# Attention and two MLPs in one launch: the written-out order and engines of the first two thirds of the steps replaced, after new step costs and a price on changes between kinds of TensorE product

## The chip, the cores and the metric

The kernel runs on one core of one Trainium2 chip. The metric is the device time of one execution in microseconds (us); less is better. The time before is the median of three runs.

## The reference

Three layers follow one another. `x` is the output of one layer and the input of the next.

```python
# attention: 4 batches, 8 heads, 576 positions, 64 per head
scores = scale * np.matmul(q, k.transpose(0, 1, 3, 2))
masks = np.stack([mask_plain if h < H // 2 else mask_dil for h in range(H)], axis=0)
scores = np.where(masks[None, :, :, :], scores, -1000000000.0)
attn = np.exp(scores - np.max(scores, axis=-1, keepdims=True))
attn = attn / (np.sum(attn, axis=-1, keepdims=True) + 1e-09)
x = np.matmul(attn, v)                 # then laid out as 2304 tokens x 512
# first MLP: 512 -> 1024 -> 512
h = x @ w_in
solu = h * softmax(h)
x = (solu - mean) / np.sqrt(var + 1e-06) * g_ln @ w_out
# second MLP: 512 -> 2048 -> 512
h = x @ w_in
x = (h * (1.0 / (1.0 + np.exp(-1.702 * h)))) @ w_out
```

`mask_plain` lets a position see the last 32 positions, `mask_dil` every fourth of the last 128. The weights arrive as 64-bit floats.

## The kernel before

**Attention.** The window is narrow, so scores are made only near the diagonal. The work is cut into 20 units n = 0 to 19, five per batch: four of two heads each, and a fifth, small one (n = 4, 9, 14, 19) for the last 64 positions of all heads. A unit goes through these steps: `att_s` makes the scores s on TensorE out of many small products (64 rows by 32 columns of the array) that follow, in the first two batches, a product of the identity with the mask; `att_max`, `att_sub` and `att_exp` work on VectorE and ScalarE; `att_sum` and `att_norm` give t on VectorE and GpSimd; `att_t` transposes t on TensorE into ptp; `att_p` copies it into diag (pt for a small unit); `att_x` multiplies with v on TensorE into xt (128 rows by 64 columns); `att_y` copies xt into the ring xr of layer input. The trace counts each of these narrow products twice.

**First MLP.** 18 token tiles of 128 rows. To keep precision every operand is split into a high and a low half, and three products are made (high by high, high by low, low by high): `moe_xh` and `moe_xl` split x, `moe_h` makes h in two halves of 12 matmuls of 512 columns each. Then follow a row maximum nm (`moe_max`, VectorE), an exponential (`moe_exp`, ScalarE), the product with h into e (`moe_solu`, VectorE), which gives h's PSUM room back, the layer norm, eight transpositions lt (`moe_lt`), their split into ln_t, and per group of three tiles the products y (`moe_y`, 24 matmuls of 384 columns each).

**Second MLP.** Three passes of 768 tokens. A two-by-two scheme with seven products instead of eight makes hx and hz (`h_prod`) and, after the activation, ox and oz (`o_prod`); sums of blocks are made before and after on VectorE, and again all operands are split in halves (gs holds the split activations, wo and w the weights). Both weight matrices of this layer are summed, split and written to DRAM (wdq, wdo) during the first MLP and read back later.

**What sets the order.** Every step is a `Work` with one or more engines that can do it and a cost in us for each (lines 946 to 1300, where `add` is called). `ORDER` is a list of the numbers of all 2,394 works. The works of one engine stand in its queue in the order of this list. `PICKS` says for a work whether it takes the second or third of its engines. `Plan.replay` (line 81) walks the queues with the costs as they are written and with rules for hops, DMA and instruction fetch; it decides in what order the works are emitted and how many filler products (`stir`, line 270) are put ahead of a product that by this reckoning has to wait. The filler works on a bank that the next product overwrites, so it only keeps TensorE at work. Each engine executes its queue strictly in this order, and waits where an input isn't there. All loads and stores go through SyncE's queue, which is in ORDER as well.

**TensorE's room.** Scores of four-head units and h share two PSUM tiles (`A`); small scores, transpositions, xt, lt and y share four banks (`B`).

Of the kernel before, what the change touches and what calls it, by code (L numbers as in the profile page):

```python
# [49 lines left out]
COLD, EARLY, LATE_RATE = 7.5, 60.0, 320e3  # L50
# [14 lines left out]
class Plan:  # L65
# [15 lines left out]
    def replay(self):  # L81
# [15 lines left out]
        port, land, lanes, ld, mms, left = 0.0, 0.0, [0.0] * LANES, 0, [], len(order)  # L97
        while left:
            best = None
            for e in QUEUES:  # L100
                if at[e] >= len(queues[e]):
                    continue
                w = queues[e][at[e]]
# [27 lines left out]
            if e == "PE":  # L131
# [7 lines left out]
                end, cost = t, w.cost * (2 if t < COLD else 1)  # L139
                for _ in range(w.mm):  # L140
# [38 lines left out]
def attention_moe_kernel(ctx, tc, qk, qk_last, v, v_last, masks, w_in, w_out, g_ln, w2_in, w2_out, out):  # L179
    nc = tc.nc  # L180
# [823 lines left out]
    for i in range(NTILE):  # L1004
# [24 lines left out]
        w = add(r, "ACT", 1.4, lambda i=i: moe_var(i), [w, z])  # L1029
        w = add(r, "POOL", 0.62, lambda i=i: moe_rs(i), [w])  # L1030
        w = add(r, "ACT", 1.4, lambda i=i: moe_ln(i), [w], port=True,
# [37 lines left out]
    for k in (1, 2, 3):  # L1069
        w_after = [end[n] for n in range(4)] if k < 3 else [closed]  # L1070
        raw, hl = (("raw", k), ("hl", k)) if k < 3 else ("raw", "hl")
        for n, u in enumerate(PARK[k]):
# [8 lines left out]
            for i in range(3):  # L1081
                w = add(r, "POOL", 0.41 if i else 0.69, lambda u=u, i=i: unit_sum(u, i, nc.gpsimd), [w], port=True,
                        also=[("DVE", 0.29 if i else 0.42, lambda u=u, i=i: unit_sum(u, i, nc.vector))])
            lo_ = None
            for part in range(2):
                fin = part == 1

                def split(copy, k=k, u=u, part=part):
# [4 lines left out]
                        also=[("DVE", 0.42 if fin else 0.35, lambda s=split: s(nc.vector.tensor_copy)),  # L1093
# [251 lines left out]
def plan_sequence():  # L1345
# [74 lines left out]
ORDER = [4, 1, 78, 79, 80, 81, 19, 88, 89, 90, 5, 8, 57, 58, 59, 60, 3, 263, 68, 91, 92, 93, 94, 262, 82, 61, 62, 0, 47, 48,  # L1420
# [239 lines left out]
```

## Time and profile before

| | us |
|---|---|
| median of 3 runs (lowest, highest) | 647.04 (646.61, 647.83) |
| profiled execution | 646.25 |
| span in it, first to last instruction | 644.5 |
| TensorE busy with matmuls | 626.5 (97%) |
| VectorE, ScalarE, GpSimd busy | 459.9, 324.2, 257.1 |
| first product of the first MLP starts at | 39.4 |
| first product of the second MLP starts at | 268.3 |
| first product of the second pass of the second MLP starts at | 402.8 |

The first line tells the metric; all other numbers are of one profiled execution, which is 0.8 us shorter than the median. The span leaves out 1.75 us around it. A timeline row gives start, length, engine, line, operation and tile; the bracket at its end tells how long the engine stood idle before it and what ended that. Lines are those of the kernel before; in the changed kernel the same statements stand four lines later.

### The profile page before, as it was taken

To read this page: it belongs to the slowest core of one execution; us is meant where nothing else is said; L and a number is where in the kernel's file an instruction comes from. 1 tells how busy PE (TensorE), PEld (TensorE's weight loads), DVE (VectorE), ACT (ScalarE), POOL (GpSimd) and SP (SyncE) were. 2 spreads that over 40 slices of the span, in tenths; PEclk is the share of its full clock that TensorE was granted. 3 is DMA by queue.
4 is the path that set the end of the run, shared out by engine and by line. 5 is a ranking of instruction groups with operands and counts; after the bars stand their busy time and mean duration, and the time that the engine had idled before them with its cause. 6 is when DMAs were issued, how large, how long until landed. Compare 5 with 4: busy or idle time off the path is not lost.

```text
span 644.5 us, 13119 instructions
## 1 busy us (share of the span) xinstructions
PE 626.5 (97%) x5065; PEld 588.8 (91%) x5065; DVE 459.9 (71%) x817; ACT 324.2 (50%) x706; POOL 257.1 (40%) x282
## 2 busy tenths in 40 slices
PE   6889999999999999999999999999999999999997
PEld 3678789889899899999999899999999999999997
DVE  3878998876787976663779969434678963448795
ACT  4689977776475564714547443322454213243331
POOL 2557546454444434655353244204123240026220
PEclk9889999999999999999999999999999999999999
DMA  8899326763667448635988998677898966868584
GB/s 319 319 376 406 116 101 221 255 212 131 216 241 255 178 149 271 235 124 174 321 291 298 343 344 296 236 253 261 275 331 261 330 206 216 290 255 296 186 262 163
DMA packets 65006, 161.36 MB, mean 250 GB/s; under 512 B 6960, under 2 KB 28592, under 8 KB 64944
## 3 DMA queue, kind: packets, MB, share of 16 engines
q1 hardware_dynamic: 64944, 160.53, 71.4%
q8 instruction: 40, 0.66, 0.4%
q14 instruction: 22, 0.18, 0.1%
HBM read 126.42 MB, written 34.08 MB: 249 GB/s over the span
## 4 chain that ended last, share of the span: by engine, by line
PE 82%; DVE 7%; DMA 4%; ACT 3%; issue 2%; POOL 1%; SPq 0%; POOLq 0%; DVEq 0%; ACTq 0%
PE y L638 15%; PE hz L762 15%; PE oz L844 14%; PE hx L762 11%; PE h L557 11%; PE ox L844 9%; PE lt L618 2%; DMA wo<-wdo 2%; DMA wdq<-hl_('q', 7, 1)_0_4305 1%; PE s L292 1%; PE xt L406 1%; DVE e L577 1%; PE ptp L377 1%; DVE gs L812 1%; DMA qk<-in_qk_dram 1%
## 5 line engine op out<-in xcount | busy, mean ns | idle before, releaser
L809 ACT CAST gs<-g 128x384 fp32r<-128x384 f32 x115 | 57.9, 513 | 87.7 <-DVE g L805 37.0
L638 PE MATMUL y<-ln_t,wo_h 128*128 128x384 f32 x384 | 98.4, 337 | 0.0
L762 PE MATMUL hz<-yc,ws 128*128 128x384 f32 x492 | 97.6, 335 | 0.0
L812 DVE TENSOR_TENSOR gs<-g,gs 128x384 fp32r<-128x384 f32 x133 | 80.2, 621 | 21.8 <-ACT gs L809 15.9
L762 PEld LDWEIGHTS hz<-yc,ws 128*128 128x128 f32 x492 | 86.3, 188 | 0.1
L762 PE MATMUL hx<-yc,ws 128*128 128x384 f32 x369 | 74.4, 335 | 0.0
L638 PEld LDWEIGHTS y<-ln_t,wo_h 128*128 128x128 f32 x384 | 69.0, 188 | 0.7
L812 POOL TENSOR_TENSOR gs<-g,gs 128x384 fp32r<-128x384 f32 x35 | 38.8, 1113 | 72.1 <-ACT gs L809 70.4
L762 PEld LDWEIGHTS hx<-yc,ws 128*128 128x128 f32 x369 | 64.8, 188 | 0.2 <-ACT p L767 0.2
L638 PE MATMUL y<-ln_t,wo_l 128*128 128x384 f32 x192 | 64.3, 335 | 0.0
L805 POOL TENSOR_TENSOR g<-g,g 128x384 f32<-128x384 f32 x25 | 28.4, 1142 | 80.2 <-DVE g L805 44.9
L557 PE MATMUL h<-wi_h,xh 128*128 128x512 f32 x144 | 59.0, 410 | 0.9 <-DVE e L577 0.9
L844 PE MATMUL ox<-gs,wo 128*128 128x384 f32 x288 | 55.7, 337 | 1.5 <-DVE gs L812 1.2
L557 PE MATMUL h<-wi_l,xh 128*128 128x512 f32 x144 | 56.6, 393 | 0.0
L557 PE MATMUL h<-wi_h,xl 128*128 128x512 f32 x144 | 56.6, 393 | 0.0
L844 PE MATMUL oz<-gs,wo 128*128 128x384 f32 x288 | 55.2, 335 | 0.1
L844 PE MATMUL oz<-gs,w 128*128 128x384 f32 x288 | 53.4, 336 | 0.0
L844 PEld LDWEIGHTS ox<-gs,wo 128*128 128x128 f32 x288 | 50.2, 188 | 3.0 <-DVE gs L812 2.5
L844 PEld LDWEIGHTS oz<-gs,wo 128*128 128x128 f32 x288 | 50.3, 188 | 0.7 <-DVE gs L812 0.7
L844 PEld LDWEIGHTS oz<-gs,w 128*128 128x128 f32 x288 | 50.1, 188 | 0.7 <-DVE gs L812 0.6
L805 DVE TENSOR_TENSOR g<-g,g 128x384 f32<-128x384 f32 x71 | 43.5, 622 | 5.9 <-ACT g L795 3.4
L795 ACT ACTIVATE g<-g 128x384 f32<-128x384 f32 x72 | 35.0, 520 | 22.6 <-DVE g L771 14.3
(420 smaller groups left out, 1203.2 us busy)
## 6 DMA issues: line engine op xcount, KB each, us to landing
wo<-wdo SPq DMA_DIRECT2D x48, 512.0 KB, 5.5
ws<-wdq SPq DMA_DIRECT2D x41, 512.0 KB, 5.4
w<-wdo SPq DMA_DIRECT2D x72, 256.0 KB, 5.1
ws<-wdq SPq DMA_DIRECT2D x41, 384.0 KB, 4.8
qk<-in_qk_dram SPq DMA_DIRECT2D x14, 528.0 KB, 7.3
v<-in_v_dram SPq DMA_DIRECT2D x14, 512.0 KB, 7.5
out_dram<-ob SPq DMA_DIRECT2D x11, 384.0 KB, 4.7
w_t<-in_w_in_dram SPq DMA_DIRECT2D x8, 512.0 KB, 7.6
```

The source lines that it names most:

```text
L292: nc.tensor.matmul(ps[QB * j:QB * j + QB, h, m * KW:m * KW + KW], q_[rows, c:c + QB], k_[rows, c:c + KW], start=not masked, stop=not maske ...
L377: nc.tensor.transpose(ps[:, j * P:j * P + P], t[:, 2 * j:2 * j + 2, :].rearrange("p m k -> p (m k)"), ident)
L406: nc.tensor.matmul(o, vW[4 * b + u][:, h, 4 * c + j, :], x, start=True, stop=True, tile_position=(0, 64 * h))
L557: nc.tensor.matmul(hps[i][:, half, :], x[:, kt, :], w[:, kt, fs], start=(kt == 0 and j == 0), stop=(kt == KT - 1 and j == 2))
L618: nc.tensor.transpose(ps[:, j, :], es[i][:, f * P:f * P + P], ident)
L638: nc.tensor.matmul(yps[g, dm][:, 0:TG].rearrange("p (t n) -> p t n", t=GT), w[:, f, ds_], x[:, :, f, :], start=(f == 0 and j == 0), stop=( ...
L762: nc.tensor.matmul(ps[:, 0:TB2], quad_weights(p, q, m, kk, a), yc2[m][:, x, kk, :], start=(m < 4 and kk == 0 and i == 0), stop=(kk == 1 an ...
L795: nc.scalar.activation(g_tile(q, 0, 0) if (half, b) == (0, 0) else src, src, AF.Gelu_apprx_sigmoid)
L805: eng.tensor_tensor(o_block(jj, *o), o_block(jj, *x), o_block(jj, *y_), op)
L809: copy(gsp[jj, m][:, 0], o_block(jj, half, b))
L812: eng.tensor_tensor(gsp[jj, m][:, 1], o_block(jj, half, b), f32(gsp[jj, m][:, 0]), ALU.subtract)
L844: nc.tensor.matmul(ps, w, gsp[jj, m][:, x], start=m < 4 and first and i == 0, stop=last and i == 2, skip_group_check=True)
```

## The change

The planner's costs and one rule are edited, and ORDER and PICKS are replaced by what a new search over them gave. No step of computation is added or taken away. The rule: when the kind of TensorE work changes from one to the next, 0.095 us are added in `replay`. Kind 2 is a work of 32 matmuls or more (scores and xt), kind 1 one of 2 or 4 (transpositions), kind 0 all others (h, y, hx, hz, ox, oz). Priced are the changes from kind 1 or 2 to 0, and from 0 to 2.

```diff
-COLD, EARLY, LATE_RATE = 7.5, 60.0, 320e3
+COLD, EARLY, LATE_RATE, TURN = 7.5, 60.0, 320e3, 0.095
...
                 end, cost = t, w.cost * (2 if t < COLD else 1)
+                kind = 2 if w.mm >= 32 else int(w.mm in (2, 4))
+                if last and not kind or kind == 2 and not last and len(mms) > 12:
+                    end += TURN
+                last = kind
...
-        w = add(r, "ACT", 1.4, lambda i=i: moe_var(i), [w, z])
-        w = add(r, "POOL", 0.62, lambda i=i: moe_rs(i), [w])
-        w = add(r, "ACT", 1.4, lambda i=i: moe_ln(i), [w], port=True,
+        w = add(r, "ACT", 1.56, lambda i=i: moe_var(i), [w, z])
+        w = add(r, "POOL", 0.55, lambda i=i: moe_rs(i), [w])
+        w = add(r, "ACT", 1.57, lambda i=i: moe_ln(i), [w], port=True,
...
-                w = add(r, "POOL", 0.41 if i else 0.69, lambda u=u, i=i: unit_sum(u, i, nc.gpsimd), [w], port=True,
+                w = add(r, "POOL", 0.43 if i else 0.86, lambda u=u, i=i: unit_sum(u, i, nc.gpsimd), [w], port=True,
...
-                        also=[("DVE", 0.42 if fin else 0.35, lambda s=split: s(nc.vector.tensor_copy)),
+                        also=[("DVE", 0.42 if fin else 0.545, lambda s=split: s(nc.vector.tensor_copy)),
...
-ORDER = [4, 1, 78, 79, 80, 81, 19, 88, 89, 90, 5, 8, 57, 58, 59, 60, 3, 263, 68, 91, 92, 93, 94, 262, 82, 61, 62, 0, 47, 48,
+ORDER = [1, 4, 78, 79, 80, 81, 82, 19, 88, 89, 90, 8, 57, 58, 59, 60, 5, 68, 91, 92, 93, 61, 62, 69, 94, 9, 267, 268, 269,
```

The first 1,600 of the 2,394 numbers of ORDER stand in a new sequence and the last 794 as before; 297 works take another engine. On TensorE the sequence of products is new up to the first product of the second pass of the second MLP, and the same from there to the end. The instructions of VectorE grow from 791 rows to 806, those of ScalarE fall from 568 to 552 and of GpSimd from 272 to 264, where alike neighbours count as one row. The fillers ahead of products fall from 15 to 11. In SyncE's queue the mask now stands first, the scores' operand of unit 1 (one piece of 528 KB) ahead of that of unit 2 (two pieces), and the third and fourth tile of w_in no longer both behind the operand of unit 6.

On TensorE in attention's first batches, the rows between unit 1's product with v and unit 0's or 2's; s is a unit's scores, ptp its transposition, xt its product with v, L274 in the kernel before a filler. Before:

```order
L406 MATMUL xt1_480<-diag0_105,v1_193 64x2x32 x16
...
L274 MATMUL ptp0_507<-ident_b_72 128x512
L377 MATMUL ptp0_507<-ident_67,t0_402 128x128 x4
...
L300 MATMUL s9_521<-mk_104,ident_b_72 128x256
L304 MATMUL s9_521<-qkl1_397 32x64 x16
L406 MATMUL xt3_546<-diag1_106,y1_early_79 64x2x32 x16
...
L292 MATMUL s7_564<-qk6_416 32x64 x32
L377 MATMUL ptp2_600<-ident_67,t2_471 128x128 x4
L406 MATMUL xt0_625<-diag0_105,v0_421 64x2x4x8 x16
```

The same place now:

```order
L410 MATMUL xt1_476<-diag0_105,v1_312 64x2x32 x16
L410 MATMUL xt3_506<-diag1_106,y1_early_79 64x2x32 x16
L381 MATMUL ptp0_529<-ident_67,t0_465 128x128 x4
L381 MATMUL ptp2_535<-ident_67,t2_375 128x128 x4
...
L308 MATMUL s9_542<-qkl1_408 32x64 x16
...
L296 MATMUL s7_564<-qk6_418 32x64 x32
...
L278 MATMUL xt2_608<-ident_b_72 128x512
L410 MATMUL xt2_608<-diag1_106,y1_early_79 64x2x4x8 x16
L410 MATMUL xt0_650<-diag0_105,v0_461 64x2x4x8 x16
```

The two products with v and the two transpositions have moved together ahead of unit 9's scores, four fillers ahead of ptp0 and one ahead of s9 are gone, and one stands ahead of xt2, which now comes before xt0.

On TensorE between the halves of the first MLP's h2 and h1 (names as above). Before:

```order
L557 MATMUL h2_900<-wi_h_95,xl2_808 128x512
L406 MATMUL xt6_998<-diag0_105,v5_820 64x2x32 x16
L292 MATMUL s13_1019<-qk11_806 32x64 x32
L377 MATMUL ptp8_1057<-ident_67,t8_729 128x128 x4
L406 MATMUL xt7_1068<-diag1_106,v6_810 64x2x4x8 x16
L557 MATMUL h1_1089<-wi_h_95,xh1_968 128x512
```

The same place now:

```order
L561 MATMUL h2_902<-wi_h_95,xl2_827 128x512
L381 MATMUL ptp6_986<-ident_67,t6_832 128x128 x4
L410 MATMUL xt7_991<-diag0_105,v6_761 64x2x4x8 x16
L296 MATMUL s13_1014<-qk11_810 32x64 x32
L381 MATMUL ptp11_1052<-ident_67,t11_894 128x128 x4
L410 MATMUL xt6_1060<-diag1_106,v5_836 64x2x32 x16
L561 MATMUL h1_1084<-wi_h_95,xh1_976 128x512
```

The transposition of unit 6, which stood inside h2, has moved to its end, so the full-width h is followed by another full-width product, and the narrow ones come behind that.

On VectorE from unit-tile 3's maximum nm3 to its e3, which frees the room of h3 (ln_t is the split transposition, t14 a small unit's masked scores, wo_l a weight split). Before:

```order
L530 SCALAR_TENSOR_TENSOR wo_l_87<-w1_t_91,g_sb_73,wo_h_86 128x512 x2
L565 TENSOR_REDUCE nm3_1297<-h3_1208 128x1
L324 TENSOR_REDUCE mx13_1327<-t13_1062 128x8
L315 SCALAR_TENSOR_TENSOR t14_1337<-s14_1310,mk_104 128x256
L324 TENSOR_REDUCE mx14_1357<-t14_1337 128x4
L625 CAST ln_t_1300<-lt0_0_1301 128x512
L577 SCALAR_TENSOR_TENSOR e3_1354,mu3_1374<-h3_1208,e3_1354 128x1024
```

The same place now:

```order
L534 SCALAR_TENSOR_TENSOR wo_l_87<-w1_t_91,g_sb_73,wo_h_86 128x512 x4
L544 CAST xh4_1302<-xr_97 128x512
L569 TENSOR_REDUCE nm3_1304<-h3_1209 128x1
L319 SCALAR_TENSOR_TENSOR t14_1339<-s14_1315,mk_104 128x256
L480 SCALAR_TENSOR_TENSOR y1_early_79<-y1_early_79 128x512
L581 SCALAR_TENSOR_TENSOR e3_1354,mu3_1363<-h3_1209,e3_1354 128x1024
```

Between nm3 and e3 stand two rows instead of four; the cast of lt0_0 has gone to ScalarE, where it stands just ahead of the exponential of h3.

## Rows read from the trace of the kernel before

**Rows 1.** The page: busy us of each engine, and the instruction queue.
```profile
PE 626.5 (97%) x5065; PEld 588.8 (91%) x5065; DVE 459.9 (71%) x817; ACT 324.2 (50%) x706; POOL 257.1 (40%) x282
...
q8 instruction: 40, 0.66, 0.4%
```

**Rows 2.** Stretches: length, busy PE, PEld, DVE, ACT, POOL; PEclk, DMA share, GB/s.
```profile
0.00:41.00 41.00, 29.56 (x834) 21.20 (x835) 26.32 (x52) 25.34 (x70) 19.46 (x27) 0.92 0.91 327
...
37.00:40.40 3.40, 3.40 (x85) 2.97 (x69) 2.56 (x4) 3.18 (x5) 1.76 (x2) 0.50 1.02 413
41.00:402.70 361.70, 358.80 (x2865) 330.71 (x2864) 281.55 (x487) 220.30 (x470) 175.58 (x193) 1.00 0.68 239
```

**Rows 3.** Timeline of TensorE in the first 40 us (columns as told above).
```profile
10.29 0.86 PE L292 MATMUL s<-qk 64*32 64x64 f32 x64 [1.62 <-DMA qk<-in_qk_dram]
...
14.80 0.44 PE L377 MATMUL ptp<-ident,t 128*128 128x128 f32 x2 [0.17 <-POOL t L369]
...
20.00 0.58 PE L288 MATMUL s<-mk,ident_b 128*128 128x256 bf16 x2 [2.07 <-DVE mx L327]
...
23.48 1.04 PE L274 MATMUL ptp<-ident_b 128*128 128x512 bf16 x4
...
29.81 1.15 PE L406 MATMUL xt<-diag,v 128*64 128x64 f32 x32 [0.88 <-DVE diag L388]
...
36.66 1.04 PE L292 MATMUL s<-qk 64*32 64x64 f32 x63 [1.83 <-issue]
...
39.40 0.78 PE L557 MATMUL h<-wi_h,xh 128*128 128x512 f32 x1
```

**Rows 4.** Timeline of GpSimd, first norm steps.
```profile
14.13 2.62 POOL L369 TENSOR_TENSOR t<-t,sx 128x256 f32<-128x256 f32 x3 [11.56 <-DVE sx L364]
```

**Rows 5.** Timeline of VectorE ahead of the product with v at 29.81.
```profile
27.44 1.39 DVE L476 SCALAR_TENSOR_TENSOR w_t<-w_t 128x1024 uint32<-128x1024 uint32 x1
...
29.08 0.67 DVE L388 COPY diag<-ptp 64x512 f32<-64x512 f32 x1
```

**Rows 6.** Timeline of TensorE where the kind of product changes.
```profile
53.52 0.39 PE L557 MATMUL h<-wi_h,xl 128*128 128x512 f32 x1
53.84 1.15 PE L406 MATMUL xt<-diag,v 128*64 128x64 f32 x32
...
57.38 0.50 PE L557 MATMUL h<-wi_h,xh 128*128 128x512 f32 x1
57.71 0.40 PE L557 MATMUL h<-wi_l,xh 128*128 128x512 f32 x1
57.95 0.39 PE L557 MATMUL h<-wi_h,xl 128*128 128x512 f32 x1
...
74.95 0.60 PE L618 MATMUL lt<-ident,e 128*128 128x128 f32 x4
75.48 0.65 PE L304 MATMUL s<-qkl 64*32 64x64 f32 x32
...
83.26 1.47 PE L618 MATMUL lt<-ident,e 128*128 128x128 f32 x12
84.57 0.60 PE L377 MATMUL ptp<-ident,t 128*128 128x128 f32 x4
84.93 0.48 PE L557 MATMUL h<-wi_h,xh 128*128 128x512 f32 x1
85.25 0.40 PE L557 MATMUL h<-wi_l,xh 128*128 128x512 f32 x1
```

**Rows 7.** Timeline around the wait at 80.42, three engines.
```profile
77.25 1.12 ACT L571 ACTIVATE e<-h,nm 128x1024 f32<-128x1024 f32 x1
...
79.05 1.22 DVE L577 SCALAR_TENSOR_TENSOR e<-h,e 128x1024 f32<-128x1024 f32 x1
...
80.42 0.47 PE L557 MATMUL h<-wi_h,xh 128*128 128x512 f32 x1 [0.92 <-DVE e L577]
```

**Rows 8.** Timeline of TensorE, a wait in the second MLP.
```profile
361.85 1.16 PE L844 MATMUL ox<-gs,wo 128*128 128x384 f32 x5 [0.57 <-DVE gs L812]
```

More of the change, by code (lines that the diff above doesn't have):

```diff
@@ L96, in replay @@
         free["SP"] = 0.75
-        port, land, lanes, ld, mms, left = 0.0, 0.0, [0.0] * LANES, 0, [], len(order)
+        port, land, lanes, ld, mms, left, last = 0.0, 0.0, [0.0] * LANES, 0, [], len(order), 0
         while left:
@@ L1535 @@
     2353, 2354, 2386, 2387, 2388, 2355, 2390, 2392, 2356, 2357, 2376, 2385, 2389, 2380, 2391, 2393]
-PICKS = {53: 1, 65: 1, 67: 1, 74: 1, 75: 1, 96: 1, 105: 1, 124: 1, 137: 1, 156: 1, 158: 1, 169: 1, 181: 1, 191: 1, 200: 1,
[24 rows of a table removed]
+PICKS = {56: 1, 64: 1, 75: 1, 85: 1, 87: 1, 94: 1, 96: 1, 97: 1, 108: 1, 116: 1, 119: 1, 127: 1, 129: 1, 137: 1, 138: 1,
[26 rows of a table added]
 _INS = ["qk", "qk_last", "v", "v_last", "masks", "w_in", "w_out", "g_ln", "w2_in", "w2_out"]
```

198 rows, old and new, of tables (ORDER, PICKS) are left out of this document.

## The prediction, made before the changed kernel ran

> **What bounds the kernel.** I read the busy times first: TensorE is at work for 97% of the span, no other engine for more than 71% [rows 1]. So the question is where TensorE stands still or runs slowly, and the table of stretches answers that. In the first 41 us it is busy for 29.56, so it idles 11.44; from 41 us to 402.7, where the sequence of its products becomes the old one again, it idles 361.70 - 358.80 = 2.90 us in all [rows 2]. After that nothing is changed on TensorE. The change can therefore win in three places: in the first 41 us, in those 2.90 us, and in products that run longer than they need. The timeline of TensorE shows what the first part consists of [rows 3]: a wait for a load (1.62 us, at 10.29), for a norm step of GpSimd (at 14.80), two stops of about 2 us (at 20.00 and 36.66), a copy of VectorE (0.88, at 29.81). In the stretch from 37.0 to 40.4 the granted clock is 0.50, the lower of its two levels, 1.2 of 2.4 GHz, right after the stop that ends at 36.66.
>
> **The stops.** The one at 36.66 is labelled issue: nothing that the profile shows was missing. The one at 20.00 names a maximum of unit 2, but the product that waits writes unit 5's scores, so I take it for the same thing. Counted along the timeline, 349 matmuls ran before the first of these and 730 before the second. The instruction queue moved 40 packets of 0.66 MB together, 16 KB each, for 5065 + 5065 matmuls and weight loads [rows 1]: 253 instructions a packet, some 127 pairs. 730 - 349 = 381 is three times 127. So TensorE runs out of instructions at a block's end if the narrow products, 63 in 1.04 us, use up a block faster than the next one comes. The product sequence of the changed kernel has the same counts up to 415 matmuls, so the stop at 20.00 stays. The block ends near 478 and 606 fall today into unit 9's scores and into xt0, and no stop is seen there. Now they fall on the last matmuls of xt3, behind xt1, with nothing wide in between, and into xt2. This is the one place where the change puts more narrow products in a row.
>
> **The change part by part.**
> *The first 15 us.* Unit 1's operand of 528 KB now passes unit 2's in SyncE's queue. At 327 GB/s in this stretch [rows 2] 540,672 bytes are 1.65 us, so the wait of 1.62 us at 10.29 goes. But what comes next is ptp of the small unit, at 14.80, and it waits for GpSimd, whose norm starts at 14.13, released by VectorE's reciprocal [rows 4]. That chain stands in the same order on VectorE and ScalarE. Unit 3's norm is now ahead of it in GpSimd's queue; GpSimd had idled for 11.56 us, and three norms take 2.62, so it should be through by then; if not, it costs its 0.9 us. I take 0 for all of this: the gain is given back at 14.80.
> *15 to 39.4 us.* Up to unit 5's scores nothing differs. Then four fillers ahead of ptp0 go, 1.04 us [rows 3], of which I count 0.9, since a matmul's end overlaps with the next one's start; xt3 and ptp2 take their place. So the same set of products (xt1, xt3, ptp0, ptp2, s9, s7) should be through 0.9 us earlier. What is late next is the first product with v after it: today xt0 at 29.81, behind a 1.39 us step on w_in and a 0.67 us copy of VectorE [rows 5]; now xt2, behind the same pair of steps, while the maximum of the small unit that stands between them (29.08 - 27.44 - 1.39 = 0.25) moves behind the copy. Then xt0 follows directly, and its copy on ScalarE now stands behind unit 9's exponential: a new wait, with ptp9, s8 and all else on TensorE queued behind it. I price it like today's in front of xt0, 0.88, so that on waits nothing is won. From there to the first h the units and the stop are the same. My value is 0.9 us earlier at 39.4. From below: 2.5 earlier, if the stop of 1.83 also falls into one of these waits. From above: 0.9 later, if a further stop of 1.83 opens at the block ends named.
> *Changes of kind.* The planner takes 0.095 us for entering wide products from any other kind, and for going from wide to narrow. Counted from the first h on, transpositions to wide fall from 22 to 16, narrow to wide from 11 to 10, wide to narrow from 11 to 4; 14 x 0.095 = 1.33 us by its price. The trace says otherwise [rows 6]. Wide to narrow: the last h takes 53.84 - 53.52 = 0.32 us instead of 0.24 (57.71 to 57.95), so 0.08. Narrow to wide: 0.33 instead of 0.24, so 0.09. Transposition to wide: four transpositions and one h take 85.25 - 84.57 = 0.68; twelve transpositions take 1.31, so four and one h would be 0.44 + 0.24 = 0.68: nothing. Transposition to narrow, which has no price in the planner: 75.48 - 74.95 = 0.53 for four, 0.09 over 0.44, and these rise from 7 to 13. The sum is -7 x 0.08 - 0.09 + 6 x 0.09 = -0.1 us. I take that; the bounds are -1.33 and, if a change between scores and products with v costs 0.09 as well (5 such places before, 7 now), +0.1.
> The Trainium skill, in TensorEngine Tiling (Array Packing), Key Properties, has a rule that speaks against the planner's price: "Changing tiling mode (not just tile) drains the TensorE". Full-width products and transpositions are one mode, the 64 by 32 scores and the products with v two others. From the first h on there are 41 changes of mode in the sequence before and 41 in the new one, so by this rule the term is 0. The rows agree with it where transpositions go to wide products.
> *The wait at 80.42.* h4 waits 0.92 us until VectorE has made e3 out of h3's room; e3 starts at 79.05, after ScalarE's exponential, which starts at 77.25 [rows 7]. Both orders have the same products on TensorE here. Between the maximum nm3 and e3 VectorE has today two steps of 512 columns and two of 256, now one of each. A copy of 512 columns takes 0.67 [rows 5]; by that, an estimate, it is 2.0 us and now 1.0, which covers the 0.92. What hides it is lt0_0's cast on ScalarE, behind which the exponential now stands: lt0_0 is done half an h earlier than needed. I take -0.9; bounds -0.9 and 0.
> *The rest.* Of the 2.90 us, 1.98 remain, 0.57 of them at one product of the second MLP, released by VectorE [rows 8]. The new sequence has other neighbours there, with costs that were corrected by some 0.15 us a step. I leave the sum as it is: 0, bounds -1.98 and +2. Moving 297 works between the vector-side engines has no price of its own: beside TensorE's 358.80 busy us they have 361.70 - 281.55 = 80 us of slack on VectorE and more on the others [rows 2].
> **Sum.** -0.9 - 0.1 - 0.9 = -1.9. Against the profiled 646.25 us that is 644.35. The median of the runs shown is 0.8 higher, 647.04, so I predict 645.1.
>
> **Rivals.**
> *All of it works.* The planner's price holds (-1.33) and its corrected costs take away the 2.90 us but for a third; with 0.9 in the first part it is -1.33 - 1.9 - 0.9 = -4.1, so 642.9. For it speaks that TensorE waits at so few places that each can be planned; against it are the rows on the changes of kind.
> *No difference.* The copy ahead of xt2 is late by as much as the fillers give, so the first h still starts near 39.4, and a new wait of about 0.9 us takes the place of that at 80.42. That leaves -0.1 to -0.5: 646.7. For it speaks that the gain at 10.29 is lost at 14.80 in just this way.
> *Slower: a fourth stop.* TensorE runs out of instructions at the end of xt3 or in xt2, 1.83 us as at 36.66, and like that one this is followed by 3.4 us at half clock, which cost 1.7. Instead of -0.9 the first part gives -0.9 + 1.83 + 1.7 = +2.6; with -0.1 and -0.9 it is +1.6: 648.6. It decides once the stop is longer than the waits it falls on by about 1 us. For it speaks the sequence; against it, that no stop is seen at 478 and 606 today.
> The Trainium skill, in Runtime: NRT & Kernel Launch, Instruction fetch mechanics, says that crossing a 16 KiB boundary is "mostly hidden". Where that held, this rival had no price and the forecast stood; the 1.83 us at 36.66 say that behind narrow products it doesn't hold here.
>
> **How the numbers follow.** Forecast 0.46, all of it 0.16, no difference 0.23, a fourth stop 0.15. This kernel's runs tell 0.2%, 1.3 us, from no change: faster is below 645.75, slower above 648.3. Faster: most of the forecast (its own range is 643.4 to 646.6, so 0.37 of 0.46), all of the first rival and a fifth of the second: 0.58. Slower: most of the fourth case, 0.13. The rest, 0.29, is the same. The low end, 642.0, lies below the first rival's middle and takes in 2.5 us in the first part with the other terms; the high end, 648.0, takes in the stop without the whole clock stretch.
>
> **What would show it.** In the timeline of the changed kernel: no wait for a load near 10, but the transposition of the small unit still at 14.8; the stop near 20 unchanged; xt2 at about 29 and the first h at 38 to 38.6. In the stretches: idle time after that up to the second pass of about 2 us instead of 2.90, and no wait for e3 ahead of h4. Wide to transposition to narrow should take as long as wide to narrow. I am wrong if the first h starts after 39.4, if the clock is at 0.50 in a third stretch, or if TensorE's idle time from 41 us on is over 4 us.

## The result: 0.5% slower, outside the range

| | us |
|---|---|
| changed kernel, median of 6 runs (lowest, highest) | 650.2 (649.71, 652.36) |
| before, median of 6 runs on the same chip | 646.83 (646.07, 648.7) |
| ratio, 95% interval | 1.0055 (1.0035, 1.0075) |
| profiled execution of the changed kernel, its span | 649.71, 647.9 |

The forecast was 645.1 in a range of 642.0 to 648.0; what came is 3.4 us slower than before. The page of the changed kernel: TensorE works as long as before, VectorE 13.7 us longer, ScalarE 13.1 us shorter, GpSimd 11.1 us longer, and the instruction queue is the same [rows 1].

```profile
PE 625.7 (97%) x5061; PEld 589.0 (91%) x5061; DVE 473.6 (73%) x838; ACT 311.1 (48%) x687; POOL 268.2 (41%) x278
...
q8 instruction: 40, 0.66, 0.4%
```

Where TensorE stands still, by stretches (length, busy PE, PEld, DVE, ACT, POOL, then PEclk, DMA share, GB/s). The changed kernel:

```profile
0.00:41.00 41.00, 28.54 (x830) 20.69 (x831) 27.31 (x52) 24.27 (x69) 18.80 (x26) 0.92 0.94 336
41.00:50.00 9.00, 7.46 (x121) 5.93 (x120) 7.98 (x15) 6.52 (x16) 3.71 (x3) 1.00 1.03 410
50.00:110.00 60.00, 56.65 (x681) 46.87 (x680) 52.80 (x83) 44.02 (x98) 43.80 (x42) 1.00 0.60 207
110.00:402.70 292.70, 291.43 (x2048) 275.16 (x2047) 231.17 (x412) 157.50 (x339) 132.46 (x141) 1.00 0.69 235
```

The kernel before, the stretches that [rows 2] does not show:

```profile
41.00:50.00 9.00, 9.00 (x128) 7.32 (x127) 6.79 (x12) 7.95 (x18) 4.39 (x4) 1.00 1.02 406
50.00:110.00 60.00, 58.93 (x790) 49.44 (x789) 54.23 (x86) 50.55 (x113) 34.58 (x36) 1.00 0.58 213
110.00:402.70 292.70, 290.87 (x1951) 273.95 (x1950) 220.54 (x391) 161.79 (x341) 136.61 (x154) 1.00 0.69 239
```

Length less busy time gives the idle time: 12.46 us now against 11.44 in the first 41 us (+1.02), 1.54 against 0 up to 50 us (+1.54), 3.35 against 1.07 up to 110 us (+2.28), 1.27 against 1.83 up to 402.7 us (-0.56). That is 4.28 us more, and 0.8 us less work, mostly four fillers: 3.5 us, the difference of the spans to 0.1. So the loss sits ahead of 110 us, and most of it behind the first h. The timeline of TensorE in the changed kernel says which waits these are (the bracket is the idle time before the row and what ended it):

```profile
9.34 0.86 PE L296 MATMUL s<-qk 64*32 64x64 f32 x64 [0.77 <-DMA qk<-in_qk_dram]
...
13.24 0.38 PE L296 MATMUL s<-y_early 64*32 64x64 f32 x18 [1.71 <-issue]
...
14.68 0.44 PE L381 MATMUL ptp<-ident,t 128*128 128x128 f32 x2 [0.73 <-POOL t L373]
...
25.04 0.33 PE L410 MATMUL xt<-diag,y_early 128*64 128x64 f32 x2 [2.53 <-issue]
...
31.44 0.62 PE L410 MATMUL xt<-diag,y_early 128*64 128x64 f32 x14 [0.97 <-issue]
...
37.85 0.24 PE L425 MATMUL xt<-pt,vl 64*64 64x32 f32 x1 [2.58 <-issue]
...
39.85 0.48 PE L561 MATMUL h<-wi_h,xh 128*128 128x512 f32 x1
...
44.73 0.68 PE L296 MATMUL s<-qk 64*32 64x64 f32 x44 [1.54 <-issue]
...
67.15 1.15 PE L410 MATMUL xt<-diag,v 128*64 128x64 f32 x32 [0.56 <-DVE diag L392]
...
76.05 0.50 PE L561 MATMUL h<-wi_h,xh 128*128 128x512 f32 x1 [0.77 <-POOL xh L544]
...
93.41 1.15 PE L410 MATMUL xt<-diag,v 128*64 128x64 f32 x32 [1.59 <-DMA v<-in_v_dram]
```

Of the two stops in [rows 3] that the prediction takes for missing instructions, the one near 20 us is gone and the one near 37 is there; new are 25.04 (behind 477 matmuls), 31.44 (behind 604) and 44.73. The kernel before has one more of them, which the prediction does not list and which stays:

```profile
13.93 0.38 PE L292 MATMUL s<-y_early 64*32 64x64 f32 x18 [1.83 <-issue]
```

In the first 50 us these stops come to 5.73 us before (1.83, 2.07, 1.83) and to 9.33 now (1.71, 2.53, 0.97, 2.58, 1.54), 3.6 more, while TensorE's waits for data there fall from 3.1 to 1.9 us, its first wait of 2.62 left out. The wait for VectorE's e at 80.42 [rows 7] is gone, and three new waits of 0.56, 0.77 and 1.59 us stand in its neighbourhood.

The half clock has moved. Before, the granted clock is 0.50 from 20.0 to 23.4 us and from 37.0 to 40.4 [rows 2]; now it is from 16.0 to 19.4 and from 26.2 to 29.6. The first of these lies on the products ahead of the block end near 20 us (eight transpositions take 1.97 us at 17.49, where they took 1.09), which reach it at 19.25, when the block is there. One row of the kernel before, two of the changed kernel:

```profile
20.00:23.40 3.40, 3.40 (x98) 2.83 (x97) 1.48 (x4) 3.28 (x11) 2.83 (x2) 0.50 1.11 363
...
16.00:19.40 3.40, 3.40 (x72) 3.10 (x64) 2.87 (x5) 2.87 (x11) 0.95 (x2) 0.50 1.07 343
26.20:29.60 3.40, 3.40 (x102) 2.04 (x100) 3.20 (x6) 1.74 (x5) 1.43 (x2) 0.50 1.02 399
```

**The stops are instruction blocks that come late.** The start of every 16 KB packet can be read from the trace's records of transfers. A block of 127 pairs of matmul and weight load is entered behind 95, 222, 349, ... matmuls, and its end is the next of these numbers; "loads" counts the transfers of SyncE's queue under way when it is entered.

```
before: block entered   7.96  13.93  20.00  25.50  30.21  36.66     changed:  7.86  13.24  19.25  25.04  31.44  37.85
next packet starts     11.71  17.53  22.93  26.80  34.35  40.58              10.92  16.42  22.66  28.86  35.52  42.44
loads under way            7      6      6      3      4      7                  8      5      7      6      4      5
TensorE goes on at     13.93  20.00      -      -  36.66      -              13.24      -  25.04  31.44  37.85  44.73
```

The sixteen profiled kernels of this study whose loads are whole (all but runs 5, 6, 17 and 18) have 114 such entries in the first 50 us. With four or more loads under way the packet starts 3.7 us after the entry (median; 8 of 10 between 2.9 and 4.5), with three or fewer 2.0 us (8 of 10 between 0.8 and 4.4, so the count alone does not settle it). Between 60 and 110 us it is 1.8 and 0.2 us. In all 48 cases of the first 50 us where TensorE stopped for over 1 us at a block's end it went on 2.20 to 2.65 us after the packet's start. So a block takes some 6 us to come while loads run, and a stop shows where 127 pairs of matmul and weight load take less. In the kernel before, the packet of the block entered at 25.50 came 1.3 us after it: SyncE issued nothing from 22 to 28 us, and the loads under way ran out at 28.9. In the changed kernel two pieces of w_in, issued at 21.15 and 22.45, run until 31.8.

**VectorE is the next limit at the end of the head.** Unit 11's scores need the room that VectorE's subtraction for unit 6 (L339, L335 before) gives, and the h of the second tile in turn the room that its mask step of unit 11 (L319, L315 before) gives. VectorE in the kernel before:

```profile
38.53 0.69 DVE L335 TENSOR_TENSOR t<-s,mx 128x512 f32<-128x512 f32 x1
39.14 1.22 DVE L476 SCALAR_TENSOR_TENSOR w_t<-w_t 128x1024 uint32<-128x1024 uint32 x1
40.28 0.69 DVE L468 TENSOR_SCALAR w_t<-w_t 128x1024 uint32<-128x1024 uint32 x1
41.07 1.23 DVE L476 SCALAR_TENSOR_TENSOR w_t<-w_t 128x1024 uint32<-128x1024 uint32 x1
43.74 0.69 DVE L315 SCALAR_TENSOR_TENSOR t<-s,mk 128x512 f32<-128x512 f32 x1 [1.44 <-PE s L292]
```

And in the changed kernel:

```profile
37.10 1.13 DVE L472 TENSOR_SCALAR w_t<-w_t 128x1024 uint32<-128x1024 uint32 x1
38.34 2.11 DVE L480 SCALAR_TENSOR_TENSOR w_t<-w_t 128x1024 uint32<-128x1024 uint32 x1
40.37 0.68 DVE L331 TENSOR_REDUCE mx<-s 128x8 f32<-128x512 f32 x1
41.16 0.69 DVE L339 TENSOR_TENSOR t<-s,mx 128x512 f32<-128x512 f32 x1
41.76 0.69 DVE L472 TENSOR_SCALAR w_t<-w_t 128x1024 uint32<-128x1024 uint32 x1
42.36 1.22 DVE L530 TENSOR_TENSOR wi_l<-w_t,wi_h 128x1024 fp32r<-128x1024 f32 x1
43.60 1.23 DVE L480 SCALAR_TENSOR_TENSOR w_t<-w_t 128x1024 uint32<-128x1024 uint32 x1
45.53 0.69 DVE L319 SCALAR_TENSOR_TENSOR t<-s,mk 128x512 f32<-128x512 f32 x1 [0.70 <-PE s L296]
```

Two more weight steps, of 1.13 and 2.11 us, now stand ahead of that subtraction, which ends at 41.85 and not at 39.22 (1.8 us of this are unit 6's scores, which end at 39.5 and not at 37.7); three stand ahead of the mask step as before. Before, VectorE waits for TensorE ahead of the mask (1.44 us) and works for 6.88 of the 10 us from 34 to 44; now it works for 10.83 of the 12 us from 34 to 46. The second tile's h starts at 46.43, where it started at 44.71. In this profile it does not wait for the mask step, which itself waits 0.70 us for scores that the stop at 44.73 made late. But VectorE is done with its weight steps only at 44.83, so without that stop no more than the 0.70 us could have been won.

### The profile page after: what moved, and what is told of

Its sections match the earlier page's. It is cut to its first block, busy times and chain, and to the rows that moved or that the text cites. A ratio compares the mean times of both kernels' runs of the same rounds, so it can differ in the third digit from the quotient of the medians.

```text
span 647.9 us, 13121 instructions
## 1 busy us (share of the span) xinstructions
PE 625.7 (97%) x5061; PEld 589.0 (91%) x5061; DVE 473.6 (73%) x838; ACT 311.1 (48%) x687; POOL 268.2 (41%) x278
## 4 chain that ended last, share of the span: by engine, by line
PE 87%; DMA 5%; POOL 3%; issue 2%; DVE 2%; SPq 1%; ACT 0%; DVEq 0%; ACTq 0%; POOLq 0%
PE y L642 16%; PE hz L766 15%; PE oz L848 14%; PE h L561 12%; PE hx L766 11%; PE ox L848 10%; PE lt L622 2%; PE xt L410 2%; DMA qk<-in_qk_dram 1%; POOL wo_h L522 1%; PE s L296 1%; PE ptp L381 1%; DMA v<-in_v_dram 1%; DMA wo<-wdo 1%; DMA ws<-wdq 1%
## 5 line engine op out<-in xcount | busy, mean ns | idle before, releaser
L816 DVE TENSOR_TENSOR gs<-g,gs 128x384 fp32r<-128x384 f32 x133 | 77.1, 597 | 18.5 <-ACT gs L813 12.6
L809 POOL TENSOR_TENSOR g<-g,g 128x384 f32<-128x384 f32 x27 | 33.0, 1227 | 99.6 <-DVE g L809 52.4
L771 ACT COPY p<-hx 128x384 f32<-128x384 f32 x24 | 11.4, 477 | 81.0 <-PE hx L766 78.1
```

What stands on the lines that cost most here:

```text
L771: nc.scalar.copy(hp1[q], hX[q][0][:, 0:TB2])
L809: eng.tensor_tensor(o_block(jj, *o), o_block(jj, *x), o_block(jj, *y_), op)
L816: eng.tensor_tensor(gsp[jj, m][:, 1], o_block(jj, half, b), f32(gsp[jj, m][:, 0]), ALU.subtract)
```

## The experiments

All times are medians of runs beside the kernel before on the same chip; the ratio is not quite that of the medians, and losses below are told from either. "Old head" is the sequence of the kernel before, "new head" that of the changed one, up to about 45 us.

| run | us | before | ratio (95%) |
|---|---|---|---|
| 1 old head, new rest | 648.56 | 646.15 | 1.0029 (1.0016, 1.0041) |
| 2 new head, old rest | 650.38 | 646.15 | 1.0060 (1.0043, 1.0078) |
| 3 old up to 68 us, new rest | 654.28 | 646.15 | 1.0110 (1.0088, 1.0132) |
| 4 changed, two waits mended | 649.61 | 646.15 | 1.0051 (1.0031, 1.0070) |
| 5 changed, thin loads, late start | 650.80 | 646.42 | 1.0078 (1.0062, 1.0094) |
| 6 before, thin loads, late start | 649.03 | 646.42 | 1.0047 (1.0030, 1.0064) |
| 7 before, one load early | 648.21 | 646.42 | 1.0026 (1.0013, 1.0039) |
| 8 changed, blocks shifted | 648.93 | 646.42 | 1.0033 (1.0019, 1.0047) |
| 9 changed, one load late | 652.23 | 646.15 | 1.0088 (1.0067, 1.0108) |
| 10 as 9, two waits mended | 650.53 | 646.15 | 1.0068 (1.0044, 1.0092) |
| 11 as 1, two waits mended | 645.54 | 646.15 | 0.9988 (0.9972, 1.0004) |
| 12 before, blocks shifted | 651.89 | 646.15 | 1.0082 (1.0067, 1.0098) |
| 13 changed again | 650.50 | 646.99 | 1.0048 (1.0029, 1.0067) |
| 14 as 4, again | 649.22 | 646.99 | 1.0033 (1.0017, 1.0049) |
| 15 as 8 and 4 together | 648.70 | 646.99 | 1.0031 (1.0018, 1.0045) |
| 16 as 11, again | 646.77 | 646.99 | 0.9993 (0.9979, 1.0006) |
| 17 changed, thin loads | 650.03 | 646.76 | 1.0049 (1.0033, 1.0065) |
| 18 before, thin loads | 644.77 | 646.76 | 0.9979 (0.9960, 0.9999) |

The changed costs and the price on changes of kind needed no run: with the old ORDER and PICKS they give the same instructions on all five engines. All of the effect is in the two tables.

**Where is it lost? Runs 1 to 4.**

```diff
 runs 1 to 3 (OLD, NEW: the two ORDERs; PICKS accordingly)
+ORDER = OLD[:146] + [w for w in NEW if w not in OLD[:146]]      # run 1; run 3 with 237
+ORDER = NEW[:146] + [w for w in OLD if w not in NEW[:146]]      # run 2
 run 4: two loads of v (37, 31: units 13 and 10) ahead of a store of split weights (741);
 tile 5's high half (392) on ScalarE
-    ..., 740, 741, 41, ..., 742, 37, ..., 31, ...
+    ..., 740, 37, 31, 741, 41, ..., 742, ...
-PICKS = {..., 392: 2, ...
```

> The changed kernel with its first 146 works (to about 45 us on TensorE, the head) in the sequence and on the engines of the kernel before; all else as changed. Theory A (two separate losses: stops of TensorE at instruction blocks in the head, 1.4 us, and new waits between 65 and 95 us, 2.3 us, less 0.4 us gained later): only the head comes back, 648.8 us. Theory B (one loss: the late head makes all that is behind it late): about 646.8 us, no difference from before. Theory C (nothing in the head matters, its stops only move): 650.2 us.

> The kernel before with its first 146 works in the sequence and on the engines of the changed kernel; all else as before. Theory A (separate losses): 648.2 us, that is the head's 1.4 us. Theory B (the head makes all late): about 650 us. Theory C (the head does not matter): 646.8 us. In the trace the instruction stops at 25, 31, 38 and 45 us should be there as in the changed kernel by A and B.

> As the first run, but with the first 237 works (to about 68 us) as in the kernel before. Theory A: the head's 1.4 us and the waits of 0.2, 0.2 and 0.6 us between 59 and 68 us come back, 647.9 us, with the waits at 76 us (GpSimd's high half of tile 5) and 93 us (the load of v) still there. Theory B: 646.8 us without these waits.

> The changed kernel with two works moved: the loads of v for units 11 and 8 go in SyncE's queue ahead of the store of a split weight part that waits for GpSimd, and the high half of tile 5 is made by ScalarE and not by GpSimd. Theory A: the waits of 0.77 us at 76 us and 1.59 us at 93 us go, 647.9 us. Theory B (they are the head's lateness seen later): other waits take their place, above 649.5 us.

The new head alone costs all of it, 3.9 us by the ratio (run 2), but with the old head 1.9 us stay (run 1). So neither theory A nor B is right as it stands, and C is wrong. In run 2 the new head's stops (2.50 at 25.53, 2.85 at 38.60) are followed by a third stretch at a granted clock of 0.50, from 40.46 to 43.87 us, on the wide products of h, and by a wait that the old rest did not have. I read it as one for PSUM room, since VectorE's e of an earlier tile ends at 58.96:

```profile
59.07 0.34 PE L296 MATMUL s<-qk 64*32 64x64 f32 x16 [1.28 <-issue]
```

In run 1 the new rest shows its own wait:

```profile
91.44 0.77 PE L410 MATMUL xt<-diag,v 128*64 128x64 f32 x19 [1.28 <-DMA v<-in_v_dram]
```

Run 3 tells nothing of the head: at its cut an lt waits 5.74 us for ScalarE's norm. Run 4's timeline has neither of the two waits, yet its time hardly differs from the changed kernel's; its profiled head was 1.8 us later (the second tile's h at 48.18), with the same instructions.

**What do the stops depend on? Runs 7, 8, 9, 12, and the thin loads.**

```diff
 run 7, the kernel before: the load of w_in's fourth tile (11) ahead of unit 6's operand (20); 15 fillers as before
-    ..., 303, 20, 109, 110, 6, 272, ..., 125, 11, 277, ...
+    ..., 303, 11, 20, 109, 110, 6, 272, ..., 125, 277, ...
 run 9, the changed kernel: the same load behind that operand, its four conversions behind load 6;
 11 fillers as in the changed kernel
-    ..., 131, 11, 277, 132, 278, ..., 279, 280, 20, 109, 110, 111, 125, 6, 273, ...
+    ..., 131, 132, ..., 20, 11, 109, 110, 111, 125, 6, 277, 278, 279, 280, 273, ...
 runs 8 and 12: ahead of the first scores
+            if n == 3:
+                plan.stirs = 2
+                for _ in range(48):
+                    nc.tensor.matmul(ps[:, 0, 0:32], ident_b, ident_b[:, 0:32], start=True, stop=True)
 runs 5, 6, 17, 18: loads of the first MLP's weights
-        nc.sync.dma_start(flat, src)
+        nc.sync.dma_start(flat[:, 0:128], src[:, 0:128])
```

Theory D says that blocks are fetched behind the loads under way, theory P that only the place of the block ends counts. (The expectations number the loads without the small units: the operand of their unit 5 is that of unit 6 here, and the loads of v for their units 11 and 8 in run 4 are those of 13 and 10.)

> The kernel before with one work of SyncE moved: the load of the fourth tile of w_in (two pieces of 512 KB) stands ahead of unit 5's operand, as in the changed kernel, and no longer behind it; all other instructions and fillers are the same. Theory D: the loads fill the pause between 22 and 28 us, so the fetch that starts at 26.8 us today (1.3 us after the block's entry) starts 1.5 to 3 us later, a new stop of about 1 us shows near 30 us at unit 0's or 1's product with v or just behind, and the time is 0.6 to 1.5 us longer, 647 to 648 us. Theory P: no new stop, no difference, 646.2 us.

> The changed kernel with the same load as in the seventh run moved the other way: the fourth tile of w_in stands behind unit 5's operand again, and the four steps on ScalarE and VectorE that turn it into 32-bit numbers stand a few places later; TensorE's instructions and all fillers are the same as in the changed kernel. Theory D (an instruction block is fetched behind the loads under way): SyncE pauses between 22 and 29 us with few loads under way, the fetch after the stop at 25 us starts 1 to 2.5 us earlier, the stop of 1.0 us at 31.4 us goes, and the time is 648 to 649.3 us. Theory P (the stops follow from where block ends stand among TensorE's products, which is not changed here): the same stops, about 650 us.

Run 7 is as theory D has it, and somewhat larger: one load moved, 1.8 us slower. TensorE stops at 26.42, where it did not (0.85 us), the packet of the block entered there starts at 29.97 instead of 26.80, and TensorE stops at that block's end too, and once more at the end of the head:

```profile
32.56 0.62 PE L406 MATMUL xt<-diag,v 128*64 128x64 f32 x14 [2.39 <-issue]
...
45.16 0.28 PE L292 MATMUL s<-qk 64*32 64x64 f32 x6 [1.70 <-issue]
```

Run 9 does to the stops what D says: those at 31.44 and 37.85 are gone, and the first h comes 2.1 us earlier, at 37.74. But unit 11's operand is now loaded behind 2 MB of weights: issued at 34.20, it lands at 43.5 (34.46 and 39.3 in the changed kernel). The time, for which D wanted 648 to 649.3, is 2 us longer than the changed kernel's:

```profile
37.74 0.47 PE L561 MATMUL h<-wi_h,xh 128*128 128x512 f32 x1
...
43.62 0.39 PE L296 MATMUL s<-qk 64*32 64x64 f32 x9 [2.87 <-DMA qk<-in_qk_dram]
```

The stretch behind that wait runs at half clock, with h in it, which takes 0.43 us a product instead of 0.24 (47.40 to 47.83 in run 9):

```profile
42.80:49.60 6.80, 5.87 (x103) 4.99 (x104) 5.87 (x10) 4.82 (x12) 3.55 (x2) 0.50 1.02 409
```

> The changed kernel with 48 short fillers (32 columns) for seven of the nine wide ones that stand ahead of the first scores, where TensorE waits for loads anyway: every block end falls 41 products earlier in the work. Theory D (blocks come at a rate while loads are under way): the stops move to other products, the first product of the first MLP comes 41/127 of about 6 us, 2 us, later, and the time is 651.5 to 652.5 us. Theory P (the place decides): the stops at 25, 31, 38 and 45 us are replaced by other ones or by none, and the time lies between 646.5 and 650.5 us.

> The kernel before with the 48 short fillers for seven of its first nine wide ones, as in the eighth run: every block end falls 41 products earlier in the work. If the place of the block ends in the old sequence is a good one (theory P), it is lost and the stops get longer: 647.5 to 649 us. If the pause in the loads is what matters (theory D), its fetch still falls into the pause and the time stays within 1 us: 645.5 to 647.2 us. A pure rate of blocks would give 648.2 us or more.

Both came out against what theory D made of them, and run 12 is slower than P had it too. The shift makes the kernel before 5.7 us slower, 651.89. It brings a stop of 4.78 us at 42.09, just ahead of h, and half clock from 41.2 to 48.0 us:

```profile
42.09 0.31 PE L425 MATMUL xt<-pt,vl 64*64 64x32 f32 x1 [4.78 <-issue]
```

In the new head the same shift saves about 1 us, with intervals that overlap. So the place of the block ends counts as much as the loads: in the kernel before, the block entered at 36.66 holds the twelve wide products of the first h, which cover the packet that comes 3.9 us late.

> The changed kernel, but of each of the sixteen 512 KB loads of the first MLP's weights only an eighth is moved (64 KB; the rest of the tile is set to zero once at the start, so its output is not the reference's); every other instruction stays. Theory D (the next instruction block is fetched behind the loads that are under way, and TensorE goes on about 2.3 us after the fetch starts): with fewer loads under way the fetch starts under 1.5 us after the block's entry and not 3 to 4.6 us, and the stops at 25, 31, 38 and 45 us shrink to under 1 us in all or go. Theory P (the stop depends on which products stand at the block's end): the stops stay at the same products, 1 to 2.6 us each. The time falls in both, since waits for weights fall: by D to 640 to 645 us.

> The same cut in the kernel before (an eighth of each weight load of the first MLP, so its output is not the reference's). By theory D the stops at 20 and 36.7 us go too, and the difference between the thin changed kernel and this one falls from 3.4 us to under 1.5 us; by theory P the stops stay and the difference stays between 2 and 4 us.

In these two the zeroing held up the first filler until 6.1 us, so their times decide nothing. Runs 17 and 18 repeat them without that:

> The fifth run again, without its late start: the changed kernel with an eighth of each 512 KB load of the first MLP's weights (its output is not the reference's); the tile is zeroed by VectorE and ScalarE ahead of their first work, so that TensorE starts at 2.6 us as in the changed kernel. Theory D (instruction blocks are fetched behind the loads under way): where fewer than five loads are under way at a block's entry its fetch starts within 2 us, and the stops between 20 and 46 us come to under 4 us in all, where the changed kernel has 7.6. Theory P (only the place counts): 7 us or more.

> The same for the kernel before (its output is not the reference's). Theory D: the stops behind 15 us (3.9 us in the kernel before) come to under 2 us, and the seventeenth run is less than 2.5 us slower than this one, since what is left are the waits behind the head (1.3 us by the thirteenth and fourteenth runs) and half the head's. Theory P: the stops stay and the difference stays at 3.5 us.

With thin loads the old head gains: 2.0 us, and in its profiled run the first h starts at 35.21 and the clock stays at 1.00 (the profiled execution is 2.1 us faster than the median). The stops that D wanted under 2 us behind 15 us come to 2.76. The new head gains nothing: 5.3 us now lie between the two, where D wanted under 2.5. Its stops between 20 and 46 us do come to 3.97, under D's 4, though one packet (entered at 20.35) still starts 3.5 us late with only three or four loads under way. Its first h comes 1.2 us earlier than in the changed kernel, but the second tile's h does not:

```profile
43.27 0.90 PE L300 MATMUL s<-qk 64*32 64x64 f32 x64 [1.68 <-issue]
...
46.97 0.47 PE L565 MATMUL h<-wi_h,xh 128*128 128x512 f32 x1 [1.73 <-DVE t L323]
```

So something other than loads and blocks also holds the new head. The starts of the first h and of the second tile's h, with VectorE's mask step ahead of the latter (us), show it:

```
new head   1st h  VectorE idle  mask ends  2nd h    old head   1st h  VectorE idle  mask ends  2nd h
changed    39.85          0.70      46.22  46.43    before     39.40          1.44      44.43  44.71
run 13     38.67             0      46.86  47.00    run 1      40.17          1.44      45.20  45.48
run 14     39.97          0.32      45.93  46.13    run 16     39.50          0.52      45.43  45.71
run 15     39.93             0      46.87  47.01    run 18     35.21             0      41.07  41.22
run 17     38.62             0      46.83  46.97
```

("idle" is VectorE's wait ahead of the mask step.) In the new head VectorE hardly waits; the first h moves by 1.4 us and the second h stays within 0.9. In runs 8, 10, 13, 15 and 17 TensorE waits for the mask step there, 0.57 to 1.76 us; in the changed kernel's first profile and in run 14 a late block comes first and VectorE stands 0.70 and 0.32 us behind it. Runs 2 and 4, whose first h came after 40.7, had the second at 47.48 and 48.18. Runs 8 to 10 lie between 46.20 and 46.86. Run 13, the changed kernel again, has other stops than the first profile and nearly the same end:

```profile
43.31 1.01 PE L296 MATMUL s<-qk 64*32 64x64 f32 x64 [1.66 <-issue]
...
47.00 0.47 PE L561 MATMUL h<-wi_h,xh 128*128 128x512 f32 x1 [1.60 <-DVE t L319]
```

No run moved VectorE's weight steps alone, so this is read from the traces and not tried.

**Are the two waits a cost of their own? Runs 10, 11, 13 to 16.** Edits as named in the table.

> The run before this one together with the two moves of the fourth run (two loads of v ahead of a store that waits for GpSimd, the high half of tile 5 on ScalarE). If the waits at 76 and 93 us cost on top of the head: 1.5 to 2.4 us less than the ninth run, 646 to 647.5 us. If other steps are late at the same time, as the fourth run's 649.6 us suggests: within 0.7 us of the ninth run.

> The first run (the old sequence up to about 45 us, the new one behind it) with the two moves of the fourth run. If what the first run still lost, 1.9 us, is the wait of 1.28 us for the load of v at 91 us and its like: 646 to 646.8 us, no difference from before. If the new sequence loses elsewhere behind 45 us: 647.5 to 648.2 us.

> The changed kernel itself, on the same chip as the three runs below, so that they can be compared with it. All theories: 650 us, 1.0035 to 1.0075 of before.

> The fourth run again (the changed kernel with the two loads of v and the high half of tile 5 moved). In the ninth and tenth runs and in the first and eleventh the two moves gave 1.7 and 2.5 us. If they act alone: 1.5 to 2.5 us less than the thirteenth run, 647.7 to 648.5 us. If they give nothing in the changed kernel: within 0.7 us of it, as the fourth run looked.

> The fourth run's two moves together with the eighth run's 48 short fillers for seven wide ones (block ends 41 products earlier in the work), in the changed kernel. If stops in the head and the two waits are separate costs, both gains add: 1.3 plus 1.7 to 2.5 us less than the thirteenth run, 646.2 to 647.2 us. If the one covers the other: 648 to 649 us.

> The eleventh run again (old sequence up to 45 us, new one behind, the two moves). Its 645.5 us were 0.12% under before with an interval that took in no change. If the new sequence behind 45 us, without its two waits, is better than the old one (the wait of 0.9 us at 80 us is gone, pass 0 waits 0.5 us less): 645 to 645.8 us. If not: 646.2 us.

Three pairs differ by the two moves alone: 9 and 10 by 1.7 us, 13 and 14 by 1.3 (a little less than the 1.5 that I expected), and 1 and 11 (or 16), which ran on different chips, by about 2.5. Each interval is about as wide as the single gain, but all three point one way, and run 4 was the odd one. With the old head and the moves nothing of the loss is left: 0.9988 and 0.9993, no difference from before that can be told. So the new sequence behind 45 us, freed of its two waits, is no better than the old one either. With the new head and the moves 2.2 us stay (run 14). Run 15 came out as its second case has it: the two gains do not add, and its second tile's h again waits for VectorE (1.76 us at 47.01). No version that computes the whole output beats the kernel before by more than the runs can tell.

## Why the prediction was wrong

- **The rest, taken as 0 with bounds of -1.98 and +2: this step failed.** Idle time from 41 to 402.7 us went from 2.90 to 6.16 us, with the 0.92 gained in it: the term was about +4.2. Two things are in it. I closed the head at the first h and counted no block end behind it; the next one, at 44.73, is a stop of 1.54 us, which the wide products of the first h had hidden before. And I wrote that moving 297 works "has no price of its own", since VectorE has 80 us of slack in 361.70. It had one: three new waits, of 0.56 for VectorE, 0.77 for GpSimd and 1.59 for a load that GpSimd held up. The slack was a mean over the whole stretch, and I looked at VectorE's order at one place, ahead of e3, and not where the head ends: there VectorE holds the second tile's h in five of the runs above.
- **The head, -0.9 with bounds of -2.5 and +0.9.** The first h came at 39.85, 0.45 us later and not 0.9 earlier; that this lies inside the bounds is luck, since up to there the stops at block ends grew by 2.1 us and the waits for data fell by 1.2. As it turned out the new head costs 2.2 us with the two waits mended (run 14) and 3.9 with the old rest (run 2), most of it behind the first h. The first 15 us went as told: 0.77 instead of 1.62 us for the load near 10, and 0.73 given back ahead of the small unit's transposition, where it was 0.17. The four fillers and 1.04 us went, but the stops came in their place.
- **The fourth stop, 0.15.** I had the place right: behind 477 and 604 matmuls TensorE stops, for 2.53 and 0.97 us. I gave it little since "no stop is seen there today", without asking what hid it. It was a pause in the loads (run 7) and the place of the ends (run 12). That the stop near 20 stays was wrong: the products ahead of it ran at half clock, and the block came in time. The half clock that this rival added did come, 0.50 from 26.2 to 29.6 us behind the stop at 25.04, but the stretch from 37.0 to 40.4 went, so there are two as before. In runs 2, 9 and 12 a stretch lay on the wide products of h. Of the rivals this one came nearest, 648.6 against 650.2, and its two stops (3.50 us) by themselves were nearly paid for by the one that went (2.07) and the shorter waits for data (1.2).
- **The wait at 80.42, -0.9.** It went, as worked out. But GpSimd's two weight steps (71.25 to 74.85) stand ahead of tile 5's high half, and GpSimd, late from there, finishes a part of the second MLP's weights at 83.67, whose store held the loads of v behind it in SyncE's queue:

```profile
71.25 3.64 POOL L522 TENSOR_SCALAR wo_h<-w_t,g_sb 128x512 fp32r<-128x512 f32 x2 [2.02 <-DVE w_t L480]
...
75.38 0.62 POOL L544 CAST xh<-xr 128x512 fp32r<-128x512 f32 x1
```

```profile
83.69 0.33 SPq L708 DMA_DIRECT2D wdq<-park_hl  x1
84.12 0.38 SPq L253 DMA_DIRECT2D qk<-in_qk_dram  x1
84.60 1.86 SPq L677 DMA_DIRECT2D y_early<-in_w_in_dram  x1
86.56 0.86 SPq L259 DMA_DIRECT2D v<-in_v_dram  x2
```

  In the kernel before the load of v for this place (unit 13) was issued at 57.48 and landed at 65.30; now it lands at 93.28, and its product starts at 93.41. Runs 10, 11 and 14 price the two new waits at 1.3 to 2.5 us.
- **Changes of kind, -0.1.** The prices hold in the changed kernel: the last h ahead of narrow products takes 0.31 us, and four transpositions ahead of narrow ones 0.53. The term is too small to be seen by itself.

```profile
70.86 0.39 PE L561 MATMUL h<-wi_h,xl 128*128 128x512 f32 x1
71.17 1.15 PE L410 MATMUL xt<-diag,v 128*64 128x64 f32 x32
...
79.18 0.60 PE L622 MATMUL lt<-ident,e 128*128 128x128 f32 x4
79.71 0.65 PE L308 MATMUL s<-qkl 64*32 64x64 f32 x32
```

- **The signs named.** Two of the three came: the first h starts after 39.4, and TensorE's idle time from 41 us on is over 4 us. There was no third stretch at half clock.
- **What is open.** The shares inside the head: how much of its 2.2 to 3.9 us are late blocks, half clock, and VectorE's room. They stand behind one another, and taking one away lets the next show (runs 9, 15, 17).

## What to carry to other kernels

Take the slack of the engine that gives back PSUM room from the very stretch where work is moved: 80 us over the whole were 1.2 us in the 12 that counted here. When a stop is absent at a block's end, find out what hides it before you move work there. A store that waits for a slow engine holds every load behind it in the same queue; move such loads ahead of it.

## What the runs showed of the hardware

- In the first 50 us a 16 KB instruction packet starts 3.7 us after the block before it is entered with four or more loads under way and 2.0 us with three or fewer (medians), and TensorE goes on 2.20 to 2.65 us after its start (48 of 48 stops of over 1 us). The Trainium skill, in Runtime: NRT & Kernel Launch, Instruction fetch mechanics, says that a crossing is "mostly hidden"; here that holds between wide products alone: behind 60 us no profile has a stop of over 1 us at a block's end.
- Forty-eight short products in place of seven wide ones, ahead of all other work, moved the time by +5.7 us in one sequence (run 12) and by about -1 us, within the noise, in another (run 8).
- The same VectorE step on a weight tile of 1024 columns took 1.23 us at 43.60 and 2.11 at 38.34, where GpSimd's split of x (1.60 us from 37.77) ran beside it.
